# Softmax attention beside a token mixer on one core: one of VectorE's four passes over a group moved to accumulating DMAs, with another rule for taking groups

## The chip, the cores and the metric

The kernel runs on one core of a Trainium2 chip. The metric is the device time of one execution in microseconds, the median of several runs. Profiles come from one profiled execution.

## What is computed

The input x is 2048 rows of 512 numbers in bf16. It is normalised row by row (xn), and the output is x + A(xn) + B(xn).

```python
# A: 32 heads of 16 columns
q, k, v = (x @ wqkv) split into heads
scores = einsum("bhqd,bhkd->bhqk", q, k) * 16 ** -0.5
o = softmax(scores) @ v          # per head
A = o (heads side by side) @ wo
# B: the mixer works along the 2048 rows
h = layernorm(x)
u = gelu(einsum("bsd,sf->bdf", h, w1) + b1)     # f = 1376
B = transpose(einsum("bdf,fs->bds", u, w2) + b2)
```

The bulk is the exponential of 32 x 2048 x 2048 scores.

## The kernel before

**Tiling.** The scores are computed transposed, keys on the 128 partitions. A block is 512 queries by 4 heads; there are 4 x 8 = 32 blocks, taken in order. Each block has 16 key tiles of 128 keys. For one key tile TensorE makes the scores of the four heads in two halves (L673, two matmuls of 128x512 each), into one of three pairs of PSUM banks. Something then has to turn each 128x1024 half into exponentials, and a matmul with V (L777, four at a time, one for each head, in four groups of columns) adds them up in one PSUM bank, numerator and denominator together, since V carries a column of ones.

**Two ways to the exponential.** On ScalarE it is one instruction for each half (`a_exp`, L752). On VectorE a whole key tile is a *group* and is made of integer and bf16 passes: two passes read PSUM and write a bf16 bit pattern as int16 into a plane of 128x2048 (`d_bits`, L961); then `d_chain` makes a second plane m of mantissa bits (`op_m`, L983), a third plane v of the bare power of two (`op_v`, L992), replaces m by the product d of the bit pattern and m (`op_d`, L1001), and adds the constant 32 to the first plane in place (`op_l`, L1009), which makes the *linear* plane. The sum of the three planes, with the linear one taken against a scaled copy VS of V, approximates the exponential, so a group costs TensorE three rounds of L777 matmuls where ScalarE's tile costs one. Planes lie in ten places: two of their own (dmore), four where x lay and four where xn lay; the last eight become free as the normalisations end.

**What sets the order.** The program is written down by a planner that runs when the kernel is built: `Dispatch` plays the five engines forward in steps of 0.01 us with the durations in `EST`, and picks, for each free engine, the ready step of lowest priority number. The order that comes out is fixed for each engine; at run time every instruction waits by semaphores for what it needs (`Sched`), and all behind it on its engine wait too. `feed` sends the scores: it calls `d_ready` and `d_next` to see whether the next scores go to VectorE as half of a group, and otherwise sends them to ScalarE. `D_KTS` lists the key tiles of a block that VectorE may take; those that it doesn't take go to ScalarE after the rest. The block's L777 rounds must all be done before the next block's start, since there is one PSUM bank for them; `pvq` holds the planes and tiles that are ready for one.

**Around it.** VectorE also evacuates the other matmuls' PSUM banks and copies each block's sums (L872); the block's denominators go by SP's DMA queue into a tile of reciprocals (L886) and back through DRAM to denb; Pool (GpSimd) multiplies sums by them (L912). That multiply is placed beside a pass of L961 where one comes up (`beside`). The mixer's matmuls and the projections are `extras`, which fill TensorE's gaps. Before the change Pool issues no DMA.

Of the kernel before, what the change touches and what calls it, by code (L numbers as in the profile page):

```python
# [35 lines left out]
NW1 = 2  # L36
NW2 = 2
QT_AT = -0.3
D_KTS = (2, 6, 10, 14)
D_FROM = 1  # L40
D_AHEAD = 7
HOLD = True
HOLD_NEED = 0.45
PV_MOST = 3
# [16 lines left out]
    exp=0.917, exp_lat=1.08, exp_pv=1.15, tanh=0.53, act_lat=0.30,  # L61
    dve_lat=0.14, p1=1.135, ts4=0.60, tt2=1.135, tt2_lat=0.115, cp512=0.60, ev_s=0.66, cp128=0.22,
    stats=0.81, norm=0.21, xcopy=0.36, small=0.16, stt=0.605, vs=0.22,
    pool_lat=0.1, rstd=1.1, pmul=1.3, sp=0.5, dma=2.6, dma_rl=4.5, dma_qp=3.0, dma_qt=7.0, dma_ot=4.5, dma_den=3.6, dma_big=6.0,
)
GATE_US = 4096 / 1200.0
GATE_MIN = 5.75
# [3 lines left out]
S_WORK = 1.0  # L71
BESIDE_US = 4.0
D_SLACK = 0.45
D_THIN = 1
LN2_BY = 64
D_PV_LATE = 0.1


class Dispatch:
# [108 lines left out]
class Sched:  # L188
# [11 lines left out]
    def add(self, eng, fn, reads=(), writes=(), name="", dma=False, extra_deps=(), out_dma=False):  # L200
        op = Op(eng, fn, name)
        op.is_dma = dma
        op.q = "o" if out_dma else "i"
        deps = set()
        for k in reads:
            w = self.last_writer.get(k)
            if w is not None:
                deps.add(w)
            if k[0] == "bank":
                for r in self.readers.get(k, ()):  # L210
                    if r.eng != eng:
                        deps.add(r)
        for k in writes:
            w = self.last_writer.get(k)
            if w is not None:
                deps.add(w)
            for r in self.readers.get(k, ()):
                deps.add(r)
        for d in extra_deps:
            if d is not None:  # L220
                deps.add(d)
        deps.discard(op)
        if eng == "pe" and not dma:
            deps = {d for d in deps if d.eng != "pe" or d.is_dma}
        op.deps = list(deps)
        for k in reads:
            self.readers.setdefault(k, []).append(op)
        for k in writes:
            self.last_writer[k] = op
            self.readers[k] = []  # L230
        op.pos = len(self.streams[eng])
        self.streams[eng].append(op)
        self.order.append(op)
        if dma:
            self.dma_ops.append(op)
        return op

    def plan(self):
        know = {e: {} for e in self.ENGS}
        sem_pools = {"i": [], "o": []}  # L240
        for op in self.order:
            K = know[op.eng]
            waits = []
            for d in sorted(op.deps, key=lambda d: -d.pos):
                if d.is_dma:
                    key = ("dma", id(d))
                    if K.get(key, -1) >= 0:
                        continue
                    waits.append(d)
                    K[key] = 0  # L250
                    for kk, vv in d.after.items():
                        if K.get(kk, -1) < vv:
                            K[kk] = vv
                else:
                    if d.eng == op.eng and not op.is_dma and d.pos >= op.pos:
                        raise AssertionError("dep on later op")
                    if K.get(d.eng, -1) >= d.pos:
                        continue
                    waits.append(d)
                    d.signals = True  # L260
                    K[d.eng] = d.pos
                    for kk, vv in d.after.items():
                        if K.get(kk, -1) < vv:
                            K[kk] = vv
            op.waits = waits
            if op.is_dma:
                chosen = None
                sem_pool = sem_pools[op.q]
                for ent in sem_pool:
                    if K.get(("dma", id(ent[2])), -1) >= 0:  # L270
                        chosen = ent
                        break
                if chosen is None:
                    chosen = [self.es.enter_context(self.nc.semaphore("dq%s%d" % (op.q, len(sem_pool)))), 0, None]
                    sem_pool.append(chosen)
                chosen[1] += 1
                chosen[2] = op
                op.dma_sem = chosen[0]
                op.dma_val = 16 * chosen[1]
                aft = dict(K)  # L280
                aft[("dma", id(op))] = 0
                op.after = aft
            else:
                aft = dict(K)
                aft[op.eng] = op.pos
                op.after = aft
        self.out_sems = [(ent[0], 16 * ent[1]) for ent in sem_pools["o"]]
        self.n_dma_sems = len(sem_pools["i"]) + len(sem_pools["o"])

    def emit(self, block, engines, sems):  # L290
        for e in self.ENGS:
# [24 lines left out]
def bass_parallel_sum__softmax_full_mha__mixer_token_mlp__prompt_kernel(  # L316
# [18 lines left out]
    with ExitStack() as es:  # L335
# [48 lines left out]
        mv = sb("mv", [128, 2 * NT, 4], F32)  # L384
        zero = sb("zero", [128, 128], BF16)
        mhalf = sb("mhalf", [128, 1], F32)
        u_sb = sb("u_sb", [128, 512], F32)
        ga_sb = sb("ga_sb", [128, 512], F32)
        osb = sb("osb", [128, 2, 512], BF16)
# [42 lines left out]
               reads=[("ident",)], writes=[("ident",)])  # L432
        sc.add("pool", lambda e: e.memset(mhalf[:], -0.5), writes=[("mhalf",)])
        sc.add("dve", lambda e: e.memset(b1c_bf[:], 0.0), writes=[("b1c",)])
        v17_main = V17[:, 0:NKT * H * 17].rearrange("p (n c) -> p n c", c=17)
        v17_kh = V17[:, 0:NKT * H * 17].rearrange("p (k h c) -> p k h c", k=NKT, c=17)
        v17_kr = V17[:, 0:NKT * H * 17].rearrange("p (k c) -> p k c", k=NKT)
# [411 lines left out]

        for k in range(NPL):  # L850
            free_at[("pl", k)] = 0.0
        d_live = {"need": 0}
        fresh = set(range(NPL))

        def planes_free():
# [79 lines left out]
        def d_pair(s_):  # L935
            u = d_next()
            if not isinstance(u, dict):
                k, keys = take_plane()
                d_live["need"] += 2
                u = dict(b=u, kt=open_d[u].pop(0), k=k, keys=keys, hf=0, n=d_state["n"])  # L940
                d_state["n"] += 1
                d_state["cur"] = u
            hf = u["hf"]
            u["hf"] += 1
            if u["hf"] == 2:
                d_state["cur"] = None
            for r in (hf, hf + 2):
                score_mm(u["b"], u["kt"], r, 2 * s_ + r // 2)
            when = dp.pe("S", EST["mm512"], S_WORK)
            scored(u["b"], 2, when)  # L950
            wait_d["n"] += 1
            p1_at.append(when)
            dp.spawn(d_bits(u, hf, s_, when))

        def d_bits(u, hf, s_, when):
            b, kt, k = u["b"], u["kt"], u["k"]

            def bits():
                if beside and dp.free["pool"] <= dp.t:
# [2 lines left out]
                                                        ps[:, s_ * 1024:(s_ + 1) * 1024],  # L962
                                                        EXP_BIAS, 0.0, ALU.add, ALU.max),
                       reads=[("bank", 2 * s_), ("bank", 2 * s_ + 1)], writes=u["keys"])
                end = dp.use("dve", EST["p1"]) + EST["dve_lat"]
                free_at[("pair", s_)] = end
                wait_d["n"] -= 1
                p1_at.pop(0)
                if hf == 1:
                    at[("bits", b, kt)] = end  # L970
                    dp.spawn(d_chain(u))
            yield ("dve", 0.0, lambda: when <= dp.t, bits)

        def d_chain(u):
            b, kt, kb = u["b"], u["kt"], u["k"]
# [3 lines left out]
            def op_m():  # L979
# [3 lines left out]
                sc.add("dve", lambda e: e.tensor_scalar(plane_i[k], plane_i[kb], 0x7F, 0x3F00,  # L983
                                                        ALU.bitwise_and, ALU.bitwise_or),
                       reads=[("pl", kb)], writes=keys)
                dp.use("dve", EST["ts4"])
            yield ("dve", pr, lambda: done(("bits", b, kt)) and planes_free(), op_m)

            def op_v():
                d_live["need"] -= 1  # L990
                k, keys = take_plane()
                sc.add("dve", lambda e: e.tensor_scalar(plane_i[k], plane_i[kb], 0x7F80, None,  # L992
                                                        ALU.bitwise_and),
                       reads=[("pl", kb)], writes=keys)
                end = dp.use("dve", EST["ts4"]) + EST["dve_lat"]
                pvq.append((b, kt, end + D_PV_LATE, ("v", k)))
            yield ("dve", pr, planes_free, op_v)

            def op_d():
                k = P["m"]  # L1000
                sc.add("dve", lambda e: e.tensor_tensor(plane_f[k], plane_f[kb], plane_f[k], ALU.mult),  # L1001
                       reads=[("pl", kb), ("pl", k)], writes=[("pl", k)])
                end = dp.use("dve", EST["tt2"])
                at[("d", b, kt)] = end + EST["tt2_lat"]
                pvq.append((b, kt, end + EST["dve_lat"] + D_PV_LATE, ("d", k)))
            yield ("dve", pr, lambda: True, op_d, EST["tt2"])

            def op_l():
                sc.add("dve", lambda e: e.tensor_scalar(plane_i[kb], plane_i[kb], LIN_S, None, ALU.add),  # L1009
                       reads=[("pl", kb)], writes=[("pl", kb)])  # L1010
                end = dp.use("dve", EST["ts4"]) + EST["dve_lat"]
                pvq.append((b, kt, end + D_PV_LATE, ("l", kb)))
            yield ("dve", pr, lambda: done(("d", b, kt)), op_l)

        d_state = {"n": 0, "cur": None}

        def d_next():
# [2 lines left out]
                return u  # L1020
            if len(planes_free()) < 1 + 2 + d_live["need"] - D_THIN:
                return None
            for b in range(pv_state["b"], min(pv_state["b"] + 2, NBLK)):
                T = blk_of(b)[2]
                if open_d[b] and len(open_a[b]) + len(open_d[b]) >= D_AHEAD and done(
                        ("QT", b), ("VS", T)) and k_ready(T, open_d[b][0]):
                    return b
            return None
# [532 lines left out]
```

## Time and profile before

| what | us |
|---|---|
| median of 3 runs (lowest, highest) | 779.49 (779.31, 780.51) |
| the profiled execution, its own time | 779.69 |
| its span, from the first to the last instruction | 777.8 |
| ScalarE busy | 748.1 |
| VectorE busy | 747.1 |
| TensorE (matmul) busy | 725.4 |
| Pool busy | 72.4 |

Busy time of an engine is the time in which at least one of its instructions runs; a matmul's end is modelled and matmuls overlap, so TensorE's figure is not its load. An instruction's mean duration includes a tail in which the next one already runs. Lines such as L961 are those of the kernel before. A row of a group names what is written and what is read, `out<-in`, then shapes, count, busy time, mean in ns, and the idle time ahead of it with its cause.

### The profile page before, as it was taken

The numbers are of one execution on the slowest core, as the hardware profiler recorded it, in microseconds if no ns is written. First come the engines' busy times: TensorE is split into PE (matmuls) and PEld (weight loads), VectorE is DVE, ScalarE is ACT, GpSimd is POOL, SyncE is SP. The second block draws the span as 40 slices with busy tenths as digits, with TensorE's granted clock in tenths as the row PEclk, the third lists the DMA queues.
The fourth block names the chain that finished last, engine by engine and source line by source line (L and its number), as shares of the span: only waits on it lengthen the run. The fifth ranks groups of instructions, "written<-read, shape, count | busy, mean of one in ns | idle before, by whom it ended". The sixth has DMA issues, their size and how long they took to land.

```text
span 777.8 us, 14344 instructions
## 1 busy us (share of the span) xinstructions
PE 725.4 (93%) x5959; PEld 210.9 (27%) x5959; DVE 747.1 (96%) x1007; ACT 748.1 (96%) x820; POOL 72.4 (9%) x110
## 2 busy tenths in 40 slices
PE   7899998999999999999989999999999999999895
PEld 3433332322222222222222222222222222222221
DVE  6789999999999999999999999999999999999995
ACT  4899999999999999999999999999999999999994
POOL 4403202000000100000000000000000000000000
PEclk9999999999999999999999999999999999999997
DMA  7502010102212103130221212202132212111001
GB/s 190 113 2 76 22 52 2 51 16 55 67 29 79 42 18 94 34 74 19 63 54 38 78 49 65 65 28 72 49 87 48 58 40 84 46 50 50 15 7 38
DMA packets 85183, 41.27 MB, mean 53 GB/s; under 512 B 61184, under 2 KB 81152, under 8 KB 85120
## 3 DMA queue, kind: packets, MB, share of 16 engines
q1 hardware_dynamic: 81952, 38.80, 18.9%
q10 hardware_dynamic: 3168, 1.57, 0.7%
q8 instruction: 46, 0.75, 0.4%
q14 instruction: 17, 0.14, 0.1%
HBM read 33.69 MB, written 5.37 MB: 50 GB/s over the span
## 4 chain that ended last, share of the span: by engine, by line
ACT 69%; DVE 19%; PE 10%; POOL 1%; DMA 1%; issue 0%; ACTq 0%; SPq 0%; DVEq 0%
ACT pT L752 68%; PE ps L673 4%; PE ps L777 3%; DVE xreg L961 2%; DVE big L961 2%; DVE stats L502 2%; PE ps L1214 2%; DVE xreg L1001 1%; DVE big L517 1%; DVE dmore L961 1%; DVE big L1001 1%; DVE big L1009 1%; DVE xreg L983 1%; DMA xreg<-in_A_x_dram 1%; DVE xreg L992 1%; DVE KT L524 1%
## 5 line engine op out<-in xcount | busy, mean ns | idle before, releaser
L752 ACT ACTIVATE pT<-ps 128x1024 bf16<-128x1024 f32 x798 | 738.3, 1099 | 9.1 <-PE ps L673 7.0
L673 PE MATMUL ps<-QT,KT 64*128 64x512 bf16 x2048 | 365.1, 385 | 31.4 <-ACT pT L752 21.6
L673 PEld LDWEIGHTS ps<-QT,KT 64*128 64x128 bf16 x2048 | 90.9, 93 | 316.2 <-ACT pT L752 234.6
L777 PE MATMUL ps<-pT,V 128*32 128x512 bf16 x1596 | 152.5, 389 | 2.4 <-ACT pT L752 2.0
L961 DVE TENSOR_SCALAR big<-ps 128x1024 int16<-128x1024 f32 x94 | 114.6, 1219 | 3.4 <-PE ps L673 2.2
L961 DVE TENSOR_SCALAR xreg<-ps 128x1024 int16<-128x1024 f32 x84 | 102.4, 1219 | 1.3 <-PE ps L673 0.4
L777 PEld LDWEIGHTS ps<-pT,V 128*32 128x32 bf16 x1596 | 39.0, 94 | 85.2 <-issue 74.3
L961 DVE TENSOR_SCALAR dmore<-ps 128x1024 int16<-128x1024 f32 x48 | 58.5, 1220 | 1.7 <-PE ps L673 1.3
L1285 PE MATMUL ps<-gT,w2blk 128*128 128x512 bf16 (+1 forms) x176 | 54.7, 385 | 0.1
L1214 PE MATMUL ps<-big,w1blk 128*128 128x512 bf16 (+1 forms) x176 | 54.4, 386 | 0.0
L912 POOL TENSOR_TENSOR oTe<-OT,denb 128x512 bf16<-128x512 f32 x15 | 19.6, 1303 | 308.8 <-DVE xreg L983 47.5
L777 PE MATMUL ps<-xreg,V 128*32 128x512 bf16 x388 | 37.6, 384 | 0.3 <-DVE xreg L1001 0.2
L912 POOL TENSOR_TENSOR oT<-OT,denb 128x512 bf16<-128x512 f32 x12 | 16.6, 1383 | 212.5 <-DMA denb<-den_scr 42.1
L1001 DVE TENSOR_TENSOR xreg<-big,xreg 128x2048 bf16<-128x2048 bf16 x27 | 33.4, 1237 | 0.0
L1009 DVE TENSOR_SCALAR big<-big 128x2048 int16<-128x2048 int16 x47 | 33.0, 703 | 0.0
L777 PE MATMUL ps<-big,V 128*32 128x512 bf16 x320 | 30.8, 384 | 1.0 <-DVE big L1001 0.6
L1009 DVE TENSOR_SCALAR xreg<-xreg 128x2048 int16<-128x2048 int16 x42 | 29.2, 695 | 0.0
L553 PE MATMUL ps<-wqkv_sb,xnT 128*128 128x128 bf16 x256 | 23.9, 224 | 1.6 <-DVE KT L524 1.4
L1001 DVE TENSOR_TENSOR big<-xreg,big 128x2048 bf16<-128x2048 bf16 x20 | 24.3, 1217 | 0.0
L872 DVE COPY OT<-ps 128x512 f32<-128x512 f32 x31 | 21.1, 681 | 0.0
L983 DVE TENSOR_SCALAR xreg<-big 128x2048 int16<-128x2048 int16 x27 | 19.7, 731 | 0.0
L777 PE MATMUL ps<-dmore,V 128*32 128x512 bf16 x196 | 19.3, 385 | 0.1
(111 smaller groups left out, 658.7 us busy)
## 6 DMA issues: line engine op xcount, KB each, us to landing
denb<-den_scr SPq DMA_DIRECT2D x31, 256.0 KB
QT<-q_img SPq DMA_DIRECT2D x15, 512.0 KB
w1blk<-in_B_w_dram SPq DMA_DIRECT2D x10, 512.0 KB
w2blk<-in_B_w_dram SPq DMA_DIRECT2D x16, 320.0 KB
w1blk<-in_A_x_dram SPq DMA_DIRECT2D x16, 128.0 KB
out_dram<-osb SPq DMA_DIRECT2D x16, 128.0 KB, 1.7
q_img<-qst SPq DMA_DIRECT2D x30, 64.0 KB
xreg<-in_A_x_dram SPq DMA_DIRECT2D x3, 512.0 KB, 11.5
```

The source lines that it names most:

```text
L553: sc.add("pe", lambda e, ct=ct: e.matmul(bank(bk)[:, 128 * j:128 * (j + 1)], lhsT=xnT[:, ct, 128 * t:128 * (t + 1)], rhs=wqkv_sb[:, ct, 2 ...
L673: sc.add("pe", lambda e: e.matmul(bank(bk), lhsT=KT[64 * (r // 2):64 * (r // 2) + 64, T, 128 * kt:128 * (kt + 1)], rhs=QT[64 * (r // 2):64 ...
L752: sc.add("act", lambda e: e.activation(pT[:, buf, :], ps[:, s_ * 1024:(s_ + 1) * 1024], ACTF.Exp, scale=EXP_SCALE), reads=[("bank", 2 * s_ ...
L777: sc.add("pe", lambda e, r=r, lhs=lhs, rhs=rhs: e.matmul(bank(PV_BANK)[32 * r:32 * r + 32, :], lhsT=lhs, rhs=rhs, start=first, stop=last, ...
L872: sc.add("dve", lambda e: e.tensor_copy(OT32[:, eb, :], bank(PV_BANK)), reads=[("bank", PV_BANK)], writes=[("OT32", eb)])
L912: sc.add("pool", lambda e: e.tensor_tensor(dst, OT32[:, eb, :], denb[:, :], ALU.mult), reads=[("OT32", eb), ("denb",)], writes=keys, extra ...
L961: sc.add("dve", lambda e: e.tensor_scalar(plane_i[k][:, 1024 * hf:1024 * (hf + 1)], ps[:, s_ * 1024:(s_ + 1) * 1024], EXP_BIAS, 0.0, ALU.a ...
L983: sc.add("dve", lambda e: e.tensor_scalar(plane_i[k], plane_i[kb], 0x7F, 0x3F00, ALU.bitwise_and, ALU.bitwise_or), reads=[("pl", kb)], wri ...
L1001: sc.add("dve", lambda e: e.tensor_tensor(plane_f[k], plane_f[kb], plane_f[k], ALU.mult), reads=[("pl", kb), ("pl", k)], writes=[("pl", k)])
L1009: sc.add("dve", lambda e: e.tensor_scalar(plane_i[kb], plane_i[kb], LIN_S, None, ALU.add), reads=[("pl", kb)], writes=[("pl", kb)])
L1214: mms = [lambda st=st: sc.add("pe", lambda e: e.matmul(bank(EX_BANK)[0:m, :], lhsT=w1blk[:, slot, st, 0:m], rhs=h_sb[:, st, :], start=(st ...
L1285: mms.append(lambda ft=ft, m=m: sc.add("pe", lambda e: e.matmul(bank(EX_BANK), lhsT=w2blk[0:m, slot, ft, :], rhs=gT[0:m, ft, :], start=(ft ...
```

## The change

The linear plane is no longer made by VectorE. `op_l` becomes a DMA on Pool's queue that adds a constant tile to the plane in place: the source is c32, 128 x 1024 int16 numbers of 32, read twice for the 2048 columns, and the addition is made by the DMA on its way. c32 is filled once by VectorE at the start. Pool's DMAs get semaphores of their own. The planner counts 1.2 us of Pool and 6.0 us more until the plane can be read.

Which groups are taken is decided anew. Before, a group was taken from the current block or the next if at least 7 of the block's tiles were still open. Now the planner keeps the VectorE work that it has promised to groups (`left`, at 4.605 us a group by its own durations); it takes none while over 3.0 us are promised, and takes one only where the group's end by its estimate lies 4 us or more ahead of the end of the exponentials left up to that block's end. One plane more must be free than before (`D_THIN`), and five tiles of a block are on offer rather than four.

```diff
-D_KTS = (2, 6, 10, 14)
+D_KTS = (2, 5, 8, 11, 14)
-D_AHEAD = 7
-    ... pmul=1.3, sp=0.5, ...
+    ... pmul=1.3, pdma=1.2, dma_lin=6.0, sp=0.5, ...
-D_THIN = 1
+D_THIN = 0
+D_COST = 2 * EST["p1"] + 2 * EST["ts4"] + EST["tt2"]
+D_LOAD = 3.0
+D_FILL = 1.0
+D_STRETCH = 1.2
+D_LATE = -4.0
...
+        c32 = sb("c32", [128, 1024], I16)
...
+        sc.add("dve", lambda e: e.memset(c32[:], 32), writes=[("c32",)])
...
             def op_l():
-                sc.add("dve", lambda e: e.tensor_scalar(plane_i[kb], plane_i[kb], LIN_S, None, ALU.add),
-                       reads=[("pl", kb)], writes=[("pl", kb)])
-                end = dp.use("dve", EST["ts4"]) + EST["dve_lat"]
+                sc.add("pool", lambda e: e.dma_start(plane_i[kb], c32[:, :].unsqueeze(1).broadcast_to([128, 2, 1024]), accum_op=ALU.add),
+                       reads=[("pl", kb), ("c32",)], writes=[("pl", kb)], name="lin", dma=True)
+                end = dp.use("pool", EST["pdma"]) + EST["dma_lin"]
                 pvq.append((b, kt, end + D_PV_LATE, ("l", kb)))
-            yield ("dve", pr, lambda: done(("d", b, kt)), op_l)
+            yield ("pool", pr, lambda: done(("d", b, kt)), op_l)
...
             if len(planes_free()) < 1 + 2 + d_live["need"] - D_THIN:
                 return None
+            load = max(0.0, dp.free["dve"] - dp.t) + d_live["left"]
+            if load > D_LOAD:
+                return None
+            fin = D_FILL + (load + D_COST) * D_STRETCH
+            ahead = max(0.0, dp.free["act"] - dp.t) + EST["exp"] * wait_a["n"]
             for b in range(pv_state["b"], min(pv_state["b"] + 2, NBLK)):
                 T = blk_of(b)[2]
-                if open_d[b] and len(open_a[b]) + len(open_d[b]) >= D_AHEAD and done(
+                ahead += 2 * EST["exp"] * (len(open_a[b]) + len(open_d[b]))
+                if open_d[b] and fin <= ahead + D_LATE and done(
                         ("QT", b), ("VS", T)) and k_ready(T, open_d[b][0]):
                     return b
```

More of the change, by code (lines that the diff above doesn't have):

```diff
@@ L63 @@
     stats=0.81, norm=0.21, xcopy=0.36, small=0.16, stt=0.605, vs=0.22,
-    pool_lat=0.1, rstd=1.1, pmul=1.3, sp=0.5, dma=2.6, dma_rl=4.5, dma_qp=3.0, dma_qt=7.0, dma_ot=4.5, dma_den=3.6, dma_big=6.0,
+    pool_lat=0.1, rstd=1.1, pmul=1.3, pdma=1.2, dma_lin=6.0, sp=0.5, dma=2.6, dma_rl=4.5, dma_qp=3.0, dma_qt=7.0, dma_ot=4.5, dma_den=3.6, dma_big=6.0,
 )
@@ L202, in add @@
         op.is_dma = dma
-        op.q = "o" if out_dma else "i"
+        op.q = "o" if out_dma else "g" if eng == "pool" else "i"
         deps = set()
@@ L239, in plan @@
         know = {e: {} for e in self.ENGS}
-        sem_pools = {"i": [], "o": []}
+        sem_pools = {"i": [], "o": [], "g": []}
         for op in self.order:
@@ L287, in plan @@
         self.out_sems = [(ent[0], 16 * ent[1]) for ent in sem_pools["o"]]
-        self.n_dma_sems = len(sem_pools["i"]) + len(sem_pools["o"])
+        self.n_dma_sems = sum(len(v) for v in sem_pools.values())
     def emit(self, block, engines, sems):
@@ L851, in bass_parallel_sum__softmax_full_mha__mixer_token_mlp__prompt_kernel @@
             free_at[("pl", k)] = 0.0
-        d_live = {"need": 0}
+        d_live = {"need": 0, "left": 0.0}
         fresh = set(range(NPL))
@@ L939, in d_pair @@
                 d_live["need"] += 2
+                d_live["left"] += D_COST
                 u = dict(b=u, kt=open_d[u].pop(0), k=k, keys=keys, hf=0, n=d_state["n"])
@@ L964, in bits @@
                        reads=[("bank", 2 * s_), ("bank", 2 * s_ + 1)], writes=u["keys"])
+                d_live["left"] -= EST["p1"]
                 end = dp.use("dve", EST["p1"]) + EST["dve_lat"]
@@ L972, in d_bits, with d_use @@
             yield ("dve", 0.0, lambda: when <= dp.t, bits)
+        def d_use(cost):
+            d_live["left"] -= cost
+            return dp.use("dve", cost)
         def d_chain(u):
@@ L985, in op_m @@
                        reads=[("pl", kb)], writes=keys)
-                dp.use("dve", EST["ts4"])
+                d_use(EST["ts4"])
             yield ("dve", pr, lambda: done(("bits", b, kt)) and planes_free(), op_m)
@@ L994, in op_v @@
                        reads=[("pl", kb)], writes=keys)
-                end = dp.use("dve", EST["ts4"]) + EST["dve_lat"]
+                end = d_use(EST["ts4"]) + EST["dve_lat"]
                 pvq.append((b, kt, end + D_PV_LATE, ("v", k)))
@@ L1002, in op_d @@
                        reads=[("pl", kb), ("pl", k)], writes=[("pl", k)])
-                end = dp.use("dve", EST["tt2"])
+                end = d_use(EST["tt2"])
                 at[("d", b, kt)] = end + EST["tt2_lat"]
@@ L1008, in op_l @@
             def op_l():
-                sc.add("dve", lambda e: e.tensor_scalar(plane_i[kb], plane_i[kb], LIN_S, None, ALU.add),
-                       reads=[("pl", kb)], writes=[("pl", kb)])
-                end = dp.use("dve", EST["ts4"]) + EST["dve_lat"]
+                sc.add("pool", lambda e: e.dma_start(plane_i[kb], c32[:, :].unsqueeze(1).broadcast_to([128, 2, 1024]), accum_op=ALU.add),
+                       reads=[("pl", kb), ("c32",)], writes=[("pl", kb)], name="lin", dma=True)
+                end = dp.use("pool", EST["pdma"]) + EST["dma_lin"]
                 pvq.append((b, kt, end + D_PV_LATE, ("l", kb)))
-            yield ("dve", pr, lambda: done(("d", b, kt)), op_l)
+            yield ("pool", pr, lambda: done(("d", b, kt)), op_l)
         d_state = {"n": 0, "cur": None}
```

## The prediction

> **What bounds the kernel now.** First the page's busy times and its chain.
>
> ```profile
> PE 725.4 (93%) x5959; PEld 210.9 (27%) x5959; DVE 747.1 (96%) x1007; ACT 748.1 (96%) x820; POOL 72.4 (9%) x110
> ...
> ACT 69%; DVE 19%; PE 10%; POOL 1%; DMA 1%; issue 0%; ACTq 0%; SPq 0%; DVEq 0%
> ```
>
> Shares over the whole span mix the start, the steady part and the end, so next the windows view for the steady part (length, then busy time of PE, PEld, DVE, ACT, POOL, clock, DMA share, GB/s), and the last long piece of the chain in order of time (start, length).
>
> ```profile
> 120.00:740.00 620.00, 590.75 (x4812) 160.96 (x4812) 614.44 (x753) 616.69 (x675) 38.72 (x33) 1.00 0.19 51
> ```
> ```profile
> 559.80 206.01 ACT pT L752 x224
> ```
>
> For 620 us ScalarE is busy 99.5% and VectorE 99.1%, and 224 exponentials stand end to end: 206.01/224 = 0.92 us each. Both engines are full, so time falls only if their joint work falls. The groups by line give that work (count | busy, mean ns):
>
> ```profile
> L752 ACT ACTIVATE pT<-ps 128x1024 bf16<-128x1024 f32 x798 | 738.3, 1099 | 9.1 <-PE ps L673 7.0
> L961 DVE TENSOR_SCALAR big<-ps 128x1024 int16<-128x1024 f32 x94 | 114.6, 1219 | 3.4 <-PE ps L673 2.2
> L1009 DVE TENSOR_SCALAR big<-big 128x2048 int16<-128x2048 int16 x47 | 33.0, 703 | 0.0
> ```
>
> 798 exponentials are 399 key tiles. L961 counts 94 + 84 + 48 = 226 over its three planes, so 113 groups, and 399 + 113 = 512 = 32 blocks of 16. Means include each instruction's tail, which overlaps its successor; the engine's pace is the distance of starts. In the timeline shown below L1001 is followed after 213.28 - 212.15 = 1.13 us and a pass such as L1009 or L983 after 0.61; L961 also after 1.13. A group holds VectorE for 2 x 1.13 (L961) + 3 x 0.60 (L983, L992, L1009) + 1.13 (L1001) = 5.2 us.
>
> **The removed pass.** L1009 goes: 113 x 0.60 = 68 us of VectorE, in a full engine. It is refilled only if the planner takes more groups. One more takes 2 x 0.92 = 1.84 us from ScalarE and costs VectorE 4.6. If both stay full, x us off the end means x/1.84 more groups and -68 + 4.6 x/1.84 = -x, so x = 68/3.5 = 19.4 us, 10.5 groups more, 123.5. The longer D_KTS offers 31 x 5 = 155, so the list is no limit.
>
> **TensorE.** Each added group brings two more rounds of four L777 matmuls, at the planner's 0.216 us a round 10.5 x 2 x 0.216 = 4.5 us in all. Nothing waits for TensorE in the long piece above, and its 22 L1114 keep-warm matmuls can give way: nothing. Without that cover 4.5 us.
>
> **The new DMA.** Pool issues it when L1001 ends; the planner expects it to land 1.2 + 6.0 = 7.2 us later and orders the VS matmul behind. The trace has no accumulating DMA and none on Pool's queue. The nearest rows move as many bytes (KB each, median us from issue to landing):
>
> ```profile
> xreg<-in_A_x_dram SPq DMA_DIRECT2D x3, 512.0 KB, 11.5
> ...
> q_img<-QT SPq DMA_DIRECT2D x2, 512.0 KB, 3.8
> ```
>
> 11.5 is among the prologue's other loads, 3.8 on a quiet queue. The addition also reads its destination, so I put it between 3.8 and 7.6, 5.7, plus 0.3 for waits of Pool: 6.0 us, inside 7.2. Both ends stay for the range. Further slack: from L1009's end to the first L777 matmul on that plane I counted a median of 0.86 us over the 113, of which the planner asked 0.24. By the Trainium skill (DMA: Bandwidth & Descriptors, Anatomy of one DMA) 2.0 us + bytes/436 GB/s, estimated, would be 3.2 us for 512 KB; no run here shows that path, and the sum by it is the same, since both land in time.
>
> **Other edits.** The DMAs share the 16 engines with SP's, busy 19% of the steady part. A reciprocal (L886) follows its block's copy (L872) by at least 5.1 us with its gather's packets done 1.6 after, so 1 to 2 us more are hidden there; some L912 multiplies start 0.5 us after denb's last packet, and a late one holds the DMA queued behind it on Pool. The memset of c32 (V's 128x512 memset took 0.49 us) lies in the first 7 us, while x loads: nothing, 0.5 if uncovered. VS grows from four to five tiles: 4 x 0.06 us.
>
> Against the ideal 19.4 I set: 1 us of tail, since D_LATE lets the last plane of a block land up to 7.2 - 4 = 3.2 us behind its last exponential; 2 us because a plane lives 7 us longer while only 6 of 10 planes are free (before some 100 us) and D_THIN = 0 asks one more; 4 us, an estimate between 0 and the rivals' prices, for holds and late landings here and there. Sum -12.4. The profiled execution took 779.69 us, its span 777.8 and 1.9 around; 779.69 - 12.4 = 767.3, and the median of the runs is 0.2 below that execution: **767.0 us**.
>
> **Rival 1, slower: Pool's descriptor writing holds VectorE.** VectorE (first fence) and Pool (second), timeline, start and us:
>
> ```profile
> 212.15 1.22 DVE L1001 TENSOR_TENSOR xreg<-big,xreg 128x2048 bf16<-128x2048 bf16 x1
> 213.28 0.68 DVE L1250 SCALAR_TENSOR_TENSOR gT<-ga_sb,u_sb 128x512 bf16<-128x512 f32 x1
> 213.88 0.69 DVE L1009 TENSOR_SCALAR big<-big 128x2048 int16<-128x2048 int16 x1
> 214.49 0.69 DVE L983 TENSOR_SCALAR xreg<-dmore 128x2048 int16<-128x2048 int16 x1
> 215.09 1.77 DVE L992 TENSOR_SCALAR big<-dmore 128x2048 int16<-128x2048 int16 x1
> ...
> 76.82 0.80 DVE L495 CAST b1col<-b1c_bf 128x11 f32<-128x11 bf16 x1
> ...
> 80.19 0.41 DVE L517 TENSOR_SCALAR big<-big,mv 128x512 bf16<-128x512 bf16 x1
> ```
> ```profile
> 214.64 1.66 POOL L912 TENSOR_TENSOR oT<-OT,denb 128x512 bf16<-128x512 f32 x1 [20.01 <-DVE big L1009]
> ...
> 76.64 0.95 POOL L488 MEMSET wo_last<- 128x1024 bf16 x1
> ...
> 80.14 0.69 POOL L508 TENSOR_TENSOR mv<-mv,mhalf 128x1 f32<-128x1 f32 x1
> ```
>
> L912 starts inside L983, is slowed (1.66 us against 1.27 for most of its 31), then runs first, and L992 takes 1.77 instead of 0.69: 1.08 us lost. A Pool memset, which only writes, made a cast of 11 columns last 0.80 us. The 128x1 operation, which writes little, held L517 not at all (0.41, as when alone). The new DMA comes just where it hurts: of 113 L1001, 59 are followed at once by the next group's L983 and then L992. If Pool's issue holds like L912, 59/113 x 1.08 = 0.56 us a group; 123.5 x 0.56 = 69 us on an engine that the plan fills, 779.5 - 19.4 + 69 = 829 us. If it holds like L508, zero. The gain is gone from 19.4/123.5 = 0.157 us a group. Descriptors are few bytes, nearer to L508, but hundreds of them, hence not a small chance. The Trainium skill (SBUF — State Buffer, Who interferes with whom) speaks against the change: a VectorE instruction that uses both ports and a GpSimd instruction exclude each other for the whole instruction, descriptor writing included. L992's 1.77 agrees for a compute instruction; by that rule this rival happens.
>
> **Rival 2, slower: it lands late.** The matmul then holds TensorE's queue, and the scores behind it feed both engines. One exponential ahead (0.92 us) covers some. With the gaps counted above, a landing at 9.3 us, 2.1 late, leaves 0.57 us a group beyond that cover: 779.5 - 19.4 + 70 = 830. It decides from about 8.7 us. For it: 11.5 under load. Against: 3.8, and 19% DMA share.
>
> **Rival 3, nothing: it takes no more groups.** Planes or the rule on remaining exponentials keep them near 113; ScalarE stays full with 798 exponentials and VectorE idles 68 us: 779 us, within 0.2%, which is about what a measurement of this kernel can tell from no change. For it: planes live longer. Against: 155 offers and D_LOAD refilling whenever under 3 us are promised.
>
> **How the numbers follow.** Forecast 0.47 (757 to 777); rival 1 0.30 (780 to 829); rival 2 0.15 (780 to 830); rival 3 0.08. So faster 0.47, same 0.08, slower 0.45. Low: the ideal, 779.5 - 19.4 = 760, with 3 us over, 757. High: rival 1 at 0.45 us a group is 779.5 - 19.4 + 55 = 815; beyond it lie some 0.17. The forecast's own range is 757 to 777.
>
> **What would show it.** Right: about 775 exponentials and 123 groups, ScalarE still over 99% from 120 to 740, L983 and L992 near 690 ns, the VS matmuls' weight loads not waiting for Pool's DMA. Wrong by rival 1: L992 means well over 0.75 us and VectorE's busy time not falling per group. By rival 2: waits of L777 for the DMA into planes, and idle ScalarE. By rival 3: some 113 groups and a VectorE with gaps. Most likely to be wrong is the cost of Pool's issue, which no row shows.

## The result, and the profile after

The changed kernel takes 812.4 us (median of 4 runs, 811.2 to 815.6) against 780.0 us for the one before in the same sessions: a ratio of 1.0419, 95% interval 1.0386 to 1.0453. It is 4.2% slower where 1.6% faster was forecast; the time lies inside the range of 757 to 815.

The page of the changed kernel, busy times and the chain's shares by engine:

```profile
PE 729.1 (90%) x6009; PEld 211.6 (26%) x6009; DVE 719.0 (89%) x925; ACT 744.1 (92%) x808; POOL 217.4 (27%) x229
...
DVE 45%; PE 22%; DMA 19%; ACT 9%; issue 2%; POOL 1%; SPq 1%; DVEq 0%; POOLq 0%
```

The steady part, same columns as before:

```profile
120.00:740.00 620.00, 567.94 (x4651) 153.12 (x4649) 567.23 (x655) 582.28 (x630) 160.90 (x133) 0.98 0.71 136
```

ScalarE fell from 99.5% to 93.9% busy, VectorE from 99.1% to 91.5%: neither is full, so the kernel is now bound by waits. The share of the DMA engines rose from 0.19 to 0.71, and 19% of the chain is DMA, where it was 1%. Line numbers moved: the exponential is L758 now, the scores L679, L777 is L783, L892 the reciprocal, L918 Pool's multiply; of a group's passes L968 reads PSUM, then L995, L1004, L1013, and L1021 is the new DMA. Two groups of the page, the exponentials and one of the linear rounds:

```profile
L758 ACT ACTIVATE pT<-ps 128x1024 bf16<-128x1024 f32 x786 | 733.9, 1065 | 43.7 <-PE ps L679 36.2
...
L783 PE MATMUL ps<-xreg,VS 128*32 128x512 bf16 x204 | 20.6, 394 | 12.2 <-DMA xreg<-c 12.2
```

There are 786 exponentials, 12 fewer, so 119 groups. ScalarE waited 36.2 us for scores (7.0 before), and the VS matmul waits for landings. The DMA view has the new queue and one of its three rows; the view of L1021 gives the landing times over all 119:

```profile
q0 software_dynamic: 32368, 62.40, 45.4%
...
xreg<-c POOLq DMA_DIRECT2D x51, 512.0 KB, 5.9
```
```profile
DMA to landing us min/median/max: 5.0/6.1/10.5
```

The median is near the estimate (5.7 us for the transfer, 6.0 with waits of Pool) and under the planned 7.2; but 29 of 119 take over 7.2 us and the longest 10.5. Other transfers suffer as well. The view of waits (total, times, longest):

```profile
DVE rl L892 <- DMA rl<-OT: 10.5, 5, 3.7
```

Five times VectorE, and all that was ordered behind L892 on it, stood for the 8 KB gather of the denominators; before, never. Counted over the 31 blocks, the gather's last packet came 1.6 us after the copy in the median before (longest 6.7) and 3.6 us now (longest 9.8). The chain in order of time shows both waits within 25 us (start, length), and the windows view what runs beside and after them:

```profile
480.16 10.45 DMA xreg<-c
490.61 0.04 issue
490.65 0.40 PE ps L783 x4
...
495.89 6.01 DMA rl<-OT
```
```profile
480.00:490.00 10.00, 8.30 (x67) 2.23 (x65) 9.79 (x10) 9.53 (x11) 4.28 (x4) 1.00 0.47 99
490.00:500.00 10.00, 9.35 (x93) 2.57 (x93) 6.29 (x8) 8.59 (x10) 1.71 (x2) 1.00 1.10 206
500.00:512.00 12.00, 8.92 (x51) 1.81 (x51) 8.16 (x10) 6.89 (x8) 1.19 (x1) 0.72 0.59 123
```

First a linear plane lands 3 us late, though the mean share of the DMA engines over those 10 us is only 0.47. Then, with the engines full (the share sums the packets' times, which overlap a little, so it can pass 1), the gather takes 6 us; VectorE and ScalarE drain, and in the next 12 us the granted clock is 0.72. Over the span the clock is below full for 47 us, 20 us before.

Beside the late plane of 480 us ran SP's 256 KB transfer that spreads the reciprocals from DRAM into denb. Its packets of 2048 bytes, the only ones of that size on SP's queue, run mostly four at a time (56% of the time in which any runs), so a mean over sixteen engines hides them. Counted over the run: of the 43 new DMAs during whose landing such packets started, 22 took over 7.2 us; of the other 76, seven did. A late spread holds linear planes in a second way too, by Pool's queue, as a later piece of the chain shows:

```profile
425.54 4.79 DMA den_scr<-rl
...
430.39 6.84 DMA denb<-den_scr
...
437.37 1.25 POOL oTe L918
438.62 5.30 DMA xreg<-c
...
443.97 0.40 PE ps L783 x4
```

Pool's multiply L918 waited for the spread, the new DMA stood behind it on Pool until 4.9 us after its L1013 had ended, and the VS matmul waited for that DMA. So the two waits are not independent.

### The profile page after: what moved, and what is told of

It reads as the page before. It is cut to its first block, busy times and chain, and to the rows that moved or that the text cites. A ratio compares the mean times of both kernels' runs of the same rounds, so it can differ in the third digit from the quotient of the medians.

```text
span 810.5 us, 14464 instructions
## 1 busy us (share of the span) xinstructions
PE 729.1 (90%) x6009; PEld 211.6 (26%) x6009; DVE 719.0 (89%) x925; ACT 744.1 (92%) x808; POOL 217.4 (27%) x229
## 3 DMA queue, kind: packets, MB, share of 16 engines
q0 software_dynamic: 32368, 62.40, 45.4%
## 4 chain that ended last, share of the span: by engine, by line
DVE 45%; PE 22%; DMA 19%; ACT 9%; issue 2%; POOL 1%; SPq 1%; DVEq 0%; POOLq 0%
PE ps L679 10%; ACT pT L758 9%; DVE xreg L968 8%; PE ps L783 7%; DMA xreg<-c 6%; DVE big L968 5%; DMA big<-c 5%; DVE xreg L1013 5%; DVE dmore L968 4%; DMA rl<-OT 3%; DVE big L1013 3%; DVE big L1004 3%; DVE xreg L995 2%; DMA denb<-den_scr 2%; DVE dmore L1013 2%
## 5 line engine op out<-in xcount | busy, mean ns | idle before, releaser
L758 ACT ACTIVATE pT<-ps 128x1024 bf16<-128x1024 f32 x786 | 733.9, 1065 | 43.7 <-PE ps L679 36.2
L679 PE MATMUL ps<-QT,KT 64*128 64x512 bf16 x2048 | 363.4, 389 | 36.6 <-ACT pT L758 17.1
L679 PEld LDWEIGHTS ps<-QT,KT 64*128 64x128 bf16 x2048 | 88.7, 93 | 316.0 <-ACT pT L758 182.3
L783 PE MATMUL ps<-pT,V 128*32 128x512 bf16 x1572 | 149.7, 391 | 1.0 <-ACT pT L758 0.6
L968 DVE TENSOR_SCALAR xreg<-ps 128x1024 int16<-128x1024 f32 x102 | 124.1, 1217 | 12.8 <-PE ps L679 11.7
L968 DVE TENSOR_SCALAR big<-ps 128x1024 int16<-128x1024 f32 x88 | 107.2, 1218 | 29.2 <-PE ps L679 28.5
L1021 POOL DMA_DIRECT2D xreg<-c x51 | 61.7, 1217 | 180.4 <-DVE big L1013 69.7
L1021 POOL DMA_DIRECT2D big<-c x44 | 53.9, 1225 | 171.8 <-DVE xreg L1013 84.3
L968 DVE TENSOR_SCALAR dmore<-ps 128x1024 int16<-128x1024 f32 x48 | 58.4, 1217 | 5.0 <-PE ps L679 4.6
L1021 POOL DMA_DIRECT2D dmore<-c x24 | 30.2, 1259 | 97.9 <-DVE xreg L1013 48.9
L783 PEld LDWEIGHTS ps<-pT,V 128*32 128x32 bf16 x1572 | 38.6, 95 | 67.9 <-issue 57.2
L783 PE MATMUL ps<-big,V 128*32 128x512 bf16 x396 | 38.3, 391 | 3.1 <-DVE big L1004 2.9
L783 PE MATMUL ps<-xreg,V 128*32 128x512 bf16 x368 | 37.0, 395 | 2.2 <-DVE OT L878 0.9
L918 POOL TENSOR_TENSOR oTe<-OT,denb 128x512 bf16<-128x512 f32 x15 | 23.5, 1568 | 30.1 <-DMA denb<-den_scr 28.3
L783 PE MATMUL ps<-xreg,VS 128*32 128x512 bf16 x204 | 20.6, 394 | 12.2 <-DMA xreg<-c 12.2
L1013 DVE TENSOR_TENSOR xreg<-big,xreg 128x2048 bf16<-128x2048 bf16 x21 | 25.5, 1216 | 0.0
L783 PE MATMUL ps<-big,VS 128*32 128x512 bf16 x176 | 17.8, 395 | 8.4 <-DMA big<-c 8.4
L1013 DVE TENSOR_TENSOR big<-xreg,big 128x2048 bf16<-128x2048 bf16 x20 | 24.4, 1220 | 0.0
```

The source lines that it names most:

```text
L679: sc.add("pe", lambda e: e.matmul(bank(bk), lhsT=KT[64 * (r // 2):64 * (r // 2) + 64, T, 128 * kt:128 * (kt + 1)], rhs=QT[64 * (r // 2):64 ...
L758: sc.add("act", lambda e: e.activation(pT[:, buf, :], ps[:, s_ * 1024:(s_ + 1) * 1024], ACTF.Exp, scale=EXP_SCALE), reads=[("bank", 2 * s_ ...
L783: sc.add("pe", lambda e, r=r, lhs=lhs, rhs=rhs: e.matmul(bank(PV_BANK)[32 * r:32 * r + 32, :], lhsT=lhs, rhs=rhs, start=first, stop=last, ...
L918: sc.add("pool", lambda e: e.tensor_tensor(dst, OT32[:, eb, :], denb[:, :], ALU.mult), reads=[("OT32", eb), ("denb",)], writes=keys, extra ...
L968: sc.add("dve", lambda e: e.tensor_scalar(plane_i[k][:, 1024 * hf:1024 * (hf + 1)], ps[:, s_ * 1024:(s_ + 1) * 1024], EXP_BIAS, 0.0, ALU.a ...
L1021: sc.add("pool", lambda e: e.dma_start(plane_i[kb], c32[:, :].unsqueeze(1).broadcast_to([128, 2, 1024]), accum_op=ALU.add), reads=[("pl", ...
```

## The experiments

Four theories. *Late*: linear planes that land after 7.2 us hold TensorE. *Crowd*: the traffic delays SP's transfers for the denominators, and VectorE's L892 and Pool's L918 wait for them. These are a chain of three: the gather of a block's denominators into rl, the put of their reciprocals into DRAM, and the spread from there into denb. *Port*: Pool's issue holds VectorE's passes. *Rule*: the new rule for taking groups is worse by itself. Kernels before gave 780.3 to 780.6 us beside these.

**The DMA not issued**, every other instruction in its place.

```diff
-                sc.add("pool", lambda e: e.dma_start(plane_i[kb], ..., accum_op=ALU.add), ...)
```

> The changed kernel with the same order of every other instruction, but the linear plane's DMA is not issued at all: the addition of 32 is left out and the matmul reads the plane as it is. It shows what the plan is worth when the DMA costs nothing. The changed kernel's 119 groups are 6 more than before, so 12 exponentials of 0.92 us fewer: 780 - 11 = 769 us if every loss comes from the DMA, be it late landings (theory late), SP's transfers crowded by its traffic (theory crowd) or Pool's issue holding VectorE (theory port). Theory rule (the new rule for taking groups makes a worse order by itself): 785 us or more.

775.0 us, ratio 0.9924 (0.9907 to 0.9940). So 37 us of the changed kernel come from the DMA. But without it the gain is 5.6 us and not the 11 that were expected. The steady part shows VectorE at 94.3%:

```profile
120.00:740.00 620.00, 575.35 (x4807) 160.16 (x4874) 584.50 (x681) 610.70 (x667) 38.31 (x32) 1.00 0.19 51
```

**TensorE waits for no landing.**

```diff
-                                pv_round(b, lambda r: VS[...], rhs, [("VS", T), ("pl", k)], last)
+                                pv_round(b, lambda r: VS[...], lambda r: xnT[:, 0, 0:512], [("VS", T)], last)
```

> The changed kernel with every DMA in its place, but the matmul with VS reads a fixed tile of xnT in place of the linear plane, so TensorE never waits for a landing (the linear term is left out of the sums). Theory late: nearly all of the 32 us comes back, 770 to 783 us. Theory crowd: VectorE's reciprocal and Pool's multiply still wait for their transfers, 795 us or more. Theory port: 800 us or more, since the issues are all there.

803.2 us, ratio 1.0290 (1.0271 to 1.0308): 9 us come back, so taking away *late* alone does little. What is left can be seen on VectorE's timeline:

```profile
580.43 1.22 DVE L968 TENSOR_SCALAR xreg<-ps 128x1024 int16<-128x1024 f32 x1
589.04 0.25 DVE L892 RECIPROCAL rl<-rl 128x16 f32<-128x16 f32 x1 [7.39 <-DMA rl<-OT]
```

One late gather idled VectorE for 7.4 us; over the run L892 waited 17.3 us.

**A small DMA with as many rows.**

```diff
-                ... e.dma_start(plane_i[kb], c32[:, :].unsqueeze(1).broadcast_to([128, 2, 1024]), accum_op=ALU.add)
+                ... e.dma_start(plane_i[kb] as (2, 1024)[:, :, 0:8], c32[:, 0:8] twice, accum_op=ALU.add)
```

> The changed kernel with the DMA over the same 128 x 2 rows but 16 bytes of each in place of 2048, so Pool has as many descriptors to write and almost no bytes move (the addition is left out for the other columns). Theories late and crowd: 768 to 778 us, since a small DMA lands early and crowds nobody. Theory port: still 800 us or more, with L995 and L1004 as slow as in the changed kernel.

782.7 us, ratio 1.0021 (1.0011 to 1.0030), between the two bands. The bytes cost 30 us; the issues by themselves, with landings of 2.7 us, cost 782.7 - 775.0 = 7.7 us. *Port* as the prediction priced it falls. The timelines of the changed kernel, VectorE and then Pool, show why:

```profile
222.63 0.68 DVE L995 TENSOR_SCALAR xreg<-dmore 128x2048 int16<-128x2048 int16 x1
223.24 0.68 DVE L1004 TENSOR_SCALAR xreg<-dmore 128x2048 int16<-128x2048 int16 x1
...
505.50 1.22 DVE L968 TENSOR_SCALAR big<-ps 128x1024 int16<-128x1024 f32 x1
506.75 0.84 DVE L995 TENSOR_SCALAR dmore<-big 128x2048 int16<-128x2048 int16 x1
```
```profile
223.01 1.22 POOL L1021 DMA_DIRECT2D xreg<-c  x1 [1.99 <-DVE big L1013]
...
505.89 1.19 POOL L1021 DMA_DIRECT2D xreg<-c  x1 [9.36 <-DVE xreg L1013]
```

At 223 the issue begins 0.38 us into L995 and spans L1004: both take 0.68 us, undisturbed, and so it was in 11 of 12 such pairs; in the twelfth, at 711, Pool's multiply ran just ahead of the issue and L995 took 1.38 us. At 506.75 L995 begins in the last third of an issue and ends 0.5 us after it, having taken 0.84 us. Counted over the run with the small DMA, the passes of L995 and L1004 exceed 0.69 us by 13.4 us in sum (4.3 without the DMA). These 9 us are about the size of the 7.7; that they are their whole cause is not shown.

**The rule alone**, linear plane on VectorE.

```diff
-                sc.add("pool", lambda e: e.dma_start(...), name="lin", dma=True)
-                end = dp.use("pool", EST["pdma"]) + EST["dma_lin"]
+                sc.add("dve", lambda e: e.tensor_scalar(plane_i[kb], plane_i[kb], LIN_S, None, ALU.add), ...)
+                end = d_use(EST["ts4"]) + EST["dve_lat"]
```

> The new rule for taking groups and the five offered tiles alone: the linear plane is made by VectorE as before (and counted in the promised work). Theory rule: slower than before, 785 us or more. Theories late, crowd and port: like before, 775 to 785 us.

782.9 us, ratio 1.0026 (1.0016 to 1.0036), with 110 groups. *Rule* explains about 2 us.

**The denominators' chain planned later**, then **the linear plane planned later**, then **both**.

```diff
-    dma_lin=6.0, ... dma_rl=4.5, ... dma_den=3.6
+    dma_lin=8.0, ... dma_rl=8.0, ... dma_den=6.0     # and the put at 4.5 for 2.6
```

> The changed kernel with later planned landings for the chain of the denominators (gather 8.0 us in place of 4.5, put 4.5 in place of 2.6, spread 6.0 in place of 3.6), so that VectorE's reciprocal and Pool's multiply are ordered where the crowded transfers have really landed; the accumulating DMA is planned as before at 1.2 + 6.0. Theory crowd through the denominators' chain: most of the loss goes, 790 us or less. Theory late (the linear planes): little changes, 805 us or more. A plan that waits longer has a price of its own, some us.

807.9 us, ratio 1.0364 (1.0312 to 1.0416), inside the band of *late* and far from that of *crowd*: 4.5 us come back. L892 waits for nothing now, but the VS matmuls wait 25.6 us for landings in place of 21.7.

> The changed kernel with the accumulating DMA planned at 1.2 + 8.0 us in place of 1.2 + 6.0, past the landing of about 95 in 100 of them. Theory late: the matmuls with VS no longer wait, 9 us or more come back as in the run where they waited for nothing (803 us or less). Theory crowd: nothing else changes, 800 to 812 us.

824.6 us, ratio 1.0566 (1.0521 to 1.0612): worse than the changed kernel, against both theories' numbers. The VS matmuls indeed hardly wait now (1.4 us), but the other wait has grown:

```profile
DVE rl L892 <- DMA rl<-OT: 32.8, 11, 8.2
```

In this order DMAs and gathers meet more often (L892 waited 11 times, not five), with 117 groups and nearly the same bytes. So *crowd* depends on where the transfers fall, and one fix alone shows little.

> The changed kernel with both planned later: the accumulating DMA at 1.2 + 8.0 us and the denominators' chain at 8.0, 4.5 and 6.0 us. Each alone gave 808 and 825 us. If the two waits (linear plane, denominators) are the whole loss, taking both into the order gives 790 us or less. If the traffic also delays what the order doesn't name (queries, stores, weights), or the longer plan costs what it saves: 800 us or more.

795.3 us, ratio 1.0194 (1.0174 to 1.0214). 17 us come back, and the time lies between the two bands. Little waiting is left (3.0 us of VS matmuls, 2.8 us of L892), so the rest probably lies in the order itself, planned around later landings with 117 groups; no run has that order without the DMA.

**Both waits gone with all the traffic**: the kernel in which the VS matmul waits for no landing, with the chain planned later.

> The run in which the VS matmul waits for no landing (803 us), with the denominators' chain planned later as well (8.0, 4.5, 6.0 us); the linear term is left out of the sums. All DMAs are issued. If late linear planes and late denominators are the loss: near the run with the small DMA, 783 to 790 us. If other delays hold: over 795 us.

781.6 us, ratio 1.0021 (1.0007 to 1.0035), with the DMA share of the steady part still at 0.72:

```profile
120.00:740.00 620.00, 584.54 (x4828) 159.75 (x4828) 580.19 (x668) 606.59 (x662) 167.53 (x135) 1.00 0.72 140
```

That is about the small DMA's 782.7, with all the traffic. So the two waits together, for the linear plane and for the denominators, are the whole loss from the bytes. The four runs side by side:

| median us | chain planned as in the change | chain planned later |
|---|---|---|
| the VS matmul waits for the plane | 812.4 | 807.9 |
| the VS matmul waits for nothing | 803.2 | 781.6 |

Either alone gives back 9.2 or 4.5 us, both together 30.8. While one wait is there, removing the other shows little, so neither has a share of its own. (The later plan is another order; its own price is in the right column.)

**The old rule with the DMA.** The kernel before with the DMA of the change and its planned cost.

> The kernel before with the accumulating DMA alone: the old rule for taking groups and the four offered tiles. Theories late and crowd: as slow as the changed kernel, 805 to 820 us, since the traffic is the same. Theory rule: clearly faster than the changed kernel, 790 us or less.

825.6 us, ratio 1.0580 (1.0542 to 1.0618), slower than either band. The new rule is worth 13 us with the DMA, so it is no part of the loss.

**Less time on the DMA engines**: a plain copy, half of the bytes, half of the DMAs.

```diff
-                ... broadcast_to([128, 2, 1024]), accum_op=ALU.add)
+                ... broadcast_to([128, 2, 1024]))
```

> The changed kernel with a plain copy of the constant tile onto the plane in place of the addition (the linear plane then holds only 32, so the linear term is left out): as many descriptors and packets of 2048 bytes from Pool's queue, but in SP's transfers a plain packet of that size takes 84 ns and here the accumulating one 186. Theories late and crowd: with half the time on the DMA engines most of the loss goes, 783 to 792 us. Theory port: as slow as the changed kernel, over 800 us.

779.5 us, ratio 0.9990 (0.9977 to 1.0002), faster than either band. The expectation was wrong in one thing: the queue carried half as many packets, of 4096 bytes, and Pool's issue took 0.72 us in place of 1.2 in the median, so some of the gain may be the issue's.

```profile
q0 software_dynamic: 17136, 62.40, 22.3%
```

The same bytes take 22.3% of the engines where the addition takes 45.4%.

> The changed kernel with 1024 of each row's 2048 bytes accumulated (the addition is left out for the other columns): as many descriptors, half the bytes. With 16 bytes it was 783 us, with all 812. Theory crowd: packets of half the time delay less and land about 1.5 us earlier, 785 to 792 us; in proportion to the bytes it would be 797 us.

783.7 us, ratio 1.0042 (1.0026 to 1.0057), with 27.3% of the engines' time: better than *crowd* expected. Half of the bytes cost 1 us over almost none, the other half 29.

> The changed kernel with the linear plane of every second group made by VectorE as before, so half as many accumulating DMAs. Theory crowd: the loss grows faster than the traffic, since a transfer is late only where two meet: 785 to 792 us, under half of the 32 us. A loss in proportion to the number of DMAs: 794 to 798 us. Faster than before only if the crowding vanishes at half the traffic: 777 us.

793.1 us, ratio 1.0167 (1.0140 to 1.0194), in none of the expected bands but nearest to the proportional one. With 22.5% of the engines it loses more than the half-sized DMAs with 27.3%: each DMA still takes as long (landing 5.6 to 6.2 us in the median). The waits show which wait is left:

```profile
PE ps L783 <- DMA big<-c: 7.7, 7, 1.7
...
DVE rl L892 <- DMA rl<-OT: 1.1, 1, 1.1
```

With the other planes the VS matmuls wait 11.1 us here (2.0 with the half-sized DMAs), and the gather costs almost nothing. Only one pair of the new DMAs overlaps in this run, yet 12 of 58 land after 7.2 us: 11 of the 24 that meet packets of the spread, and one of the other 34. So late planes go with the spread even where no other new DMA is near; that the spread is the cause is not shown, since no run changes it.

**What the gain could have been.** Three kernels without the DMA: the plane counted as ready at once; the same with groups taken later in a block; the old rule.

```diff
-    pdma=1.2, dma_lin=6.0        # first and second kernel
+    pdma=0.1, dma_lin=0.0
-D_LATE = -4.0                    # second kernel only
+D_LATE = 4.0
```

> As the run without the DMA (775 us, 119 groups), and the planner counts no time for the linear plane either (it is readable when L1013 ends): 120 groups. The addition of 32 is left out. If the planned 7.2 us of landing is what kept that run's gain at 5.5 us in place of 19.4 (matmuls and planes waiting at the ends of blocks): 766 to 771 us. If the number of groups is the limit: 773 to 776 us.

768.2 us, ratio 0.9847 (0.9824 to 0.9870), 120 groups. The planned landing time alone cost 775.0 - 768.2 = 6.8 us.

> As e14_free_no_latency, with groups taken until later in a block (D_LATE = 4.0 in place of -4.0): 125 groups, about as many as the sum in the prediction asked for. The addition of 32 is left out. If the number of groups is the limit: 760 to 765 us, the ideal of 779.5 - 19.4. If VectorE's work at the ends of blocks is late and TensorE waits there: 768 us or more.

771.9 us, ratio 0.9899 (0.9879 to 0.9920), 125 groups. More groups do not help: ScalarE now waits 12.1 us for L783 to free its buffers, 1.2 us in the kernel above.

```profile
L758 ACT ACTIVATE pT<-ps 128x1024 bf16<-128x1024 f32 x774 | 718.1, 1064 | 21.4 <-PE ps L783 12.1
```

> The old rule for taking groups with four offered tiles and no DMA issued, the planner still counting 1.2 + 6.0 us for the plane: 117 groups. The addition of 32 is left out. With the DMA it was 826 us. If the new rule is better by itself where the plane comes late: 778 us or more, against 775 of the new rule. If the rules are equal: 773 to 777 us.

780.6 us, ratio 1.0005 (0.9993 to 1.0017). With a late plane the old rule gains nothing.

No kernel that computes the whole and uses the DMA came under the kernel before.

## Why the prediction was wrong

**The bound and the ideal.** That both engines were full was read rightly. The step to 19.4 us and 123.5 groups failed: it let VectorE stay full, and the order does not. Even with a free and instant plane the kernel takes 120 groups and gains 12.4 us, and 125 groups are slower. With the planned landing of 7.2 us it gains 5.6: that lateness by plan cost 6.8 us, against 1 us of tail and 2 us for planes that live longer in the sum.

**The 4 us "for holds and late landings": the term that failed most.** The DMA itself cost 812.4 - 775.0 = 37.4 us: 7.7 with almost no bytes, and 29.7 more with all of them. Two steps led to so small a term, one for each of the two waits.

**The new DMA.** The landing was estimated well in the median and priced as if all landed so ("both land in time"). A quarter took over 7.2 us. Removing the wait for it gave back 9.2 us by itself, and 26.3 us (807.9 to 781.6) where the denominators were planned later too.

**Other edits.** "1 to 2 us more are hidden there", of the denominators' gather and spread. That took the gather's median of 1.6 us, though its longest before was already 6.7, and the DMA's bytes were never turned into time on the engines. From the rows after, q0 takes 45.4% of 810.5 us, 368 us, over 119 DMAs: 3.1 us of all sixteen engines each. So the gather's tail went to 9.8 us, past the 5.1 after which the earliest reciprocal is ordered, and VectorE's fixed order made each late gather a stop for all behind it. The late spread held Pool and the next linear plane, as the sum's own remark on Pool's queue foresaw without a price. Planning the chain later gave back 4.5 us by itself, and 21.6 us (803.2 to 781.6) where no matmul waited for a plane.

**Rival 1** has a true kernel and a wrong size: 7.7 us and not 69. Of the rows it leaned on, Pool's multiply and memset were the wrong neighbours. Its count was off too: of the 59 L983 right behind an L1001, only 28 have L992 next (L1009 left out), and in the changed kernel L995 and L1004 follow L1013 in 13 of 119. By the Trainium skill (SBUF — State Buffer, Who interferes with whom) the exclusion lasts the whole instruction; the passes of 0.68 us inside an issue of 1.2 us disagree, the 0.84 us at its end shows that a part of it does exclude.

**Rival 2** named the right chain, a matmul that holds TensorE's queue, and its signs came: VS matmuls that wait 21.7 us for the DMA, and idle ScalarE. It decided on the landing's mean, where the tail decides, and it had only one of the two waits. **Rival 3** was partly so: 119 groups, not 113.

**The chances** gave slower 0.45. That the range held the time is luck: its upper end, 815, was rival 1 at 0.45 us a group, which did not happen.

From the kernel before to the changed one, by the differences of the runs: 780.4, -5.4 for the removed pass under the new order, +7.7 for Pool's issues with small DMAs, +29.7 for the bytes by the two waits, 812.4 us.

## What to carry to other kernels

Work that is moved to DMA is not free because it is asynchronous: turn its bytes into time on the DMA engines, add it to the share they have, and ask which other transfer with a reader in a fixed order stands behind it. Compare the tail of the landing, not its median, with the planned time, for the new DMA and for those already there. Here a wait that was hidden by 3 us at 19% of the engines was bare at 71%. And look beside the mean share: the slowest landing came at a share of 0.47. When two waits are in one order, remove them one by one and together before giving either a share.

## What the runs showed of the hardware

An accumulating DMA of 512 KB within SBUF, as it went out here in packets of 2048 bytes, holds the engines twice as long as a plain copy of the same bytes in packets of 4096 (45.4% against 22.3%) and lands in 5.0 us at best against 3.1. Pool's issue of 256 rows takes 1.2 us with rows of 16, 1024 or 2048 bytes. VectorE's fast passes that began in its first half took at most 0.74 us; in its second half they took up to 0.86. By the Trainium skill (DMA: Bandwidth & Descriptors, Issuing engines are not separate DMA queues) transfers of all queues interleave on the same sixteen engines; the gather on SP's queue, 1.6 us before and 3.6 us beside Pool's queue, agrees.
